# Tile addresses, one load on another queue and two whole iotas in a one-core attention and gated-feed-forward kernel

## The chip, the cores and the metric

The kernel runs on one core of a Trainium2 chip. The metric is the device time of one execution in microseconds (us). Fifteen executions before the change have a median of 226.3 us and lie between 226.01 and 227.61 us. One execution was also recorded by the hardware profiler, and all the lines shown below come from that one.

A core has five engines that work beside each other: PE (TensorE, matrix products; its weight loads are listed as PEld), DVE (VectorE), ACT (ScalarE), POOL (GpSimd) and SP (SyncE, which only issues transfers here). Data moves between the memory of the chip (DRAM) and the on-chip memory (SBUF, 128 partitions) by DMA. A transfer is issued from the instruction stream of SP, ACT or POOL, and then runs on the core's 16 DMA engines. In this kernel every transfer that changes fp32 to bf16 on its way is issued by POOL.

## The reference

Inputs are q, k, v of shape (4 batches, 8 heads, 768 positions, 64), one decay `lam` per head, and three weight matrices. The first half is causal linear attention with decay, in blocks of positions:

```python
intra = einsum('bhic,bhjc->bhij', qb, kb) * Dmask      # lam ** (i - j) where i >= j, else 0
intra = einsum('bhij,bhjd->bhid', intra, vb)
inter = einsum('bhid,bhde->bhie', qb * lam_pow, kv_state)
out[:, :, sl] = intra + inter
kv_state = lam_block * kv_state + einsum('bhsd,bhse->bhde', kb * rev_pow, vb)
```

Its output, as x of shape (3072 tokens, 512), goes through a gated feed-forward layer:

```python
gate = 1 / (1 + exp(-(x @ w_gate)))     # w_gate: 512 x 1536
val = x @ w_val                         # w_val:  512 x 1536
out = (gate * val) @ w_out              # w_out: 1536 x 512
```

## The kernel before

**The steps.** The 768 positions are worked in six steps n = 0 to 5 of 128 positions for all four batches, which makes 512 tokens a step. Attention of a step (`piece_s`, `piece_m`, `piece_a`, and from step 2 the `chunk_` functions) leaves x transposed in the tile `XT`. The feed-forward part (`piece_gv`) then takes twelve slices of 128 columns: for each slice ft four matmuls with `WG` into the gate, four with `WV` into the value (both L484), a sigmoid on ACT and a product on DVE. `piece_po` multiplies the twelve results with `WO` (L519) and stores. From the second half of step 0's feed-forward on, the attention of the next step is put between the matmuls of the present one, so that PE has work while ACT and DVE prepare operands.

**The order.** The scheduling is manual: each engine runs its instructions in the order in which the kernel's lines emit them, and waits only on semaphores for data. So the order of POOL's list is the order of the lines, transfers included.

**The start.** Only step 0 has nothing to overlap with. Its loads are issued in this order:

- SP: batches 0 and 1 of k, as fp32 into the two `h32` tiles (`load_hw`, L150, called on L154 and L155), which DVE then casts to bf16 (`cast_hw`, L289).
- ACT: the decays, `lam_bc`; after that the table for exp and log (L157).
- POOL: q of batches 0 and 1 (L94), the identity and three tables (iotas and selects, up to L170), k of batches 2 and 3, four small iotas into `jn` (L174), a select (L176), q of batch 2, q of batch 3, v of batches 0 and 1, of 2, of 3, and then the weight slices `WG` (L105) and `WV` (L108), alternating; later `WO` (L115) and the loads of steps 1 and 2.

`jn` holds two exponents for each partition, one column for a decay that counts down from the start of a half of 64 rows and one for a decay that counts to its end. It is read only in `tables_late` on ACT (L218, L219).

PE waits in `zeros` (L533, matmuls on zeros) and then takes each batch in turn: `t_` transposes q and k (L263), `e_q` and `e_k` copy the result to SBUF (DVE L271 for q of batch 0, ACT L271 and L284 for the others), `piece_s` makes scores (L306), `piece_m` masks them on DVE (L314), `piece_a` multiplies with v (L337; batch 3 in two parts, L580), and `piece_x` and the lines after it copy to `XT` (ACT L350 and L583, DVE L350 and L584). The first gate product of step 0 is done in two halves, batches 0 and 1 first.

**Later loads.** From step 2 on, q and k are loaded to tiles and then transposed by a transfer from SP (`xbar`, L294). `gate` (L611) puts a one-column copy on POOL that waits for these transposes, and v of the same step is loaded after it.

**Addresses.** Tiles are placed in SBUF by pool, and within a pool in the order in which the code creates them, each rounded up to 32 bytes for a partition. Four constants of 32 bytes each follow the first 16,384 bytes, so that the first tile of the pool `const`, `WG`, starts at byte 16,512, which is 128 past a multiple of 256. `WV`, `WO` and `ident` have sizes that are multiples of 256 and also start 128 past one. The small tiles behind them end with `gates` (4 bytes, rounded to 32) at 64,512, and the pools after `const`, with `kb`, `qb`, `vb`, `h32`, `qt`, `kt`, `XT`, `ob` and all others in them, start at 64,544: every one of these tiles starts 32 past a multiple of 256. A row of 64 bf16 elements that a load of q, k or v writes is 128 bytes long.

Of the kernel before, what the change touches and what calls it, by code (L numbers as in the profile page):

```python
# [8 lines left out]
FP32 = mybir.dt.float32  # L9
BF16 = mybir.dt.bfloat16  # L10
# [6 lines left out]
def kernel(  # L17
# [11 lines left out]
    nc = tc.nc  # L29

    B, H, S, D = q.shape
    C = 128
# [9 lines left out]
    const = ctx.enter_context(tc.tile_pool(name="const", bufs=1))  # L42
# [18 lines left out]
    L = C // 2  # L61
    SYNC = mybir.DependencyInfo(mybir.DependencyClass.Sync, mybir.DependencyReason.DATA)

    WG = const.tile([128, NMT, DFF], BF16, tag="WG")
    WV = const.tile([128, NMT, DFF], BF16, tag="WV")
    WO = const.tile([128, NFT, DM], BF16, tag="WO")
# [15 lines left out]
    def rows_of(u):  # L82
        return slice(u * 64, (u + 1) * 64)

    def load(n, what, b0=0, b1=B):
        sl = slice(n * C, (n + 1) * C)
        for c in what:
            if (c, n) not in T_:
                T_[c, n] = qkv.tile([128, B, H, D], BF16, tag=c + "b", name=c + "b",
                                      bufs=5 if c == "v" else 4)  # L90
            src = {"q": q, "k": k, "v": v}[c]
            nat = b1 if n == 0 or c == "v" else min(b1, NB2)
            if b0 < nat:
                nc.gpsimd.dma_start(  # L94
                    out=T_[c, n][:, b0:nat],
                    in_=src[b0:nat, :, sl, :].rearrange("b h s d -> s (b h) d"))
            if nat < b1:
                m = max(nat, b0)
                for u in range(2):
                    nc.gpsimd.dma_start(  # L100
                        out=T_[c, n][:, m:b1, u::2, :],
                        in_=src[m:b1, 1 - u::2, sl, :].rearrange("b h s d -> s (b h) d"))

    def load_g(f0, f1):
        nc.gpsimd.dma_start(out=WG[:, :, f0 * 128:f1 * 128], in_=wg_r[:, :, f0 * 128:f1 * 128])  # L105

# [25 lines left out]
    jn = const.tile([128, 2], FP32, tag="jn")  # L132
# [14 lines left out]
    def load_hw(c, b, eng):  # L147
        src = {"q": q, "k": k}[c]
        H32[c, b] = hwp.tile([128, H, D], FP32, tag="h32", name="h32")
        eng.dma_start(out=H32[c, b], in_=src[b, :, 0:C, :].rearrange("h s d -> s h d"))  # L150

    T_["k", 0] = qkv.tile([128, B, H, D], BF16, tag="kb", name="kb", bufs=4)
    load_hw("k", 0, nc.sync)
    load_hw("k", 1, nc.sync)  # L154
    nc.scalar.dma_start(out=lam_bc, in_=lam.partition_broadcast(128))  # L155
    load(0, "q", 0, 2)
    nc.scalar.preload_act_table_set("natural_log_exp_and_others")  # L157
    nc.vector.memset(ident, 0.0)
# [5 lines left out]
    for u in range(2):  # L164
# [4 lines left out]
                            pattern=[[1, C]], channel_multiplier=-1)  # L169
    nc.gpsimd.iota(ip1, pattern=[[1, C]], base=1, channel_multiplier=0,  # L170
                   allow_small_or_imprecise_dtypes=True)
    load(0, "k", 2, 4)
    for u, i, base in ((0, 0, -1), (1, 0, -1), (0, 1, L - 1), (1, 1, L - 1)):
        nc.gpsimd.iota(jn[rows_of(u), i:i + 1], pattern=[[0, 1]], base=base, channel_multiplier=-1,  # L174
                       allow_small_or_imprecise_dtypes=True)
    nc.gpsimd.affine_select(out=tri, in_=tri, compare_op=ALU.is_gt, fill=1.0, base=0,  # L176
                            pattern=[[-1, C]], channel_multiplier=1)
# [8 lines left out]
    load_v(4, 5)  # L186
    load_v(5, 6)

    lns = const.tile([128, 2 * H], FP32, tag="lns")
    lnl, lnp = lns[:, 0:H], lns[:, H:2 * H].rearrange("p (i h) -> p i h", i=2)  # L190
    nc.scalar.activation(lnl, lam_bc, AF.Ln)
    for i in range(2):
# [3 lines left out]
    lamq, lamqs = lamq2[:, 0], lamq2[:, 1]  # L196
    for hp in range(HP):
        nc.scalar.activation(lamq[:, hp, :], ip1, AF.Exp, scale=lnp[:, 0, hp:hp + 1])
    pk = const.tile([128, 2, H], FP32, tag="pk")
    kds = const.tile([128, 2, H], FP32, tag="kds")  # L200
    pow_l = const.tile([128, 2 * H], FP32, tag="pow_l")
    dec_l = pow_l[:, H:2 * H].rearrange("p (i h) -> p i h", i=2)
# [10 lines left out]

    def powers(u):
        nc.scalar.activation(mask0[:, u], mask0[:, u], AF.Exp)

    def tables_late():
        nc.scalar.activation(pk[:, 1], lnl, AF.Exp, scale=jn[:, 0:1])  # L218
        nc.scalar.activation(kds[:, 1], lnl, AF.Exp, scale=jn[:, 1:2])  # L219
        nc.scalar.activation(pow_l, lns, AF.Exp, scale=float(L))  # L220
# [38 lines left out]
    def t_(c, n, bs, pool=ps_at, tag="ps"):  # L259
        ps = pool.tile([128, len(bs), HP, C], BF16, name="t" + c, tag=tag)  # L260
        for i, b in enumerate(bs):
            for hp in range(HP):
                nc.tensor.transpose(ps[:, i, hp, :], T_[c, n][:, b, 2 * hp:2 * hp + 2, :], ident)  # L263
        (tqs if c == "q" else tks)[n, bs[0]] = ps

    def e_q(n, bs, eng=None):
        w = len(bs)
        src = tqs[n, bs[0]] if n < FIRST_XBAR else QT[n][:, bs[0]:bs[0] + w]
        t = trsb.tile([128, 2, HP, C], BF16, tag="QS", name="QS")
        if n == 0:  # L270
# [205 lines left out]
    def piece_gv(n, ft):  # L476
# [54 lines left out]
    def zeros(m):  # L531
        for _ in range(m):
            nc.tensor.matmul(zps, lhsT=ST[1, 0][:, 0, 0], rhs=ST[1, 0][:, 0], start=True, stop=True)  # L533

    zeros(9)
    exponents(0)
    powers(0)
    cast_hw("k", 0)
    t_("k", 0, [0])
    e_k(0, [0])  # L540
    exponents(1)
    cast_hw("k", 1)
    zeros(3)
    powers(1)
    t_("q", 0, [0])
    e_q(0, [0], nc.vector)
    t_("q", 0, [1])
# [56 lines left out]
    load(1, "v", 2, 4)  # L604
    load(2, "qk")

    gates = const.tile([128, 2], BF16, tag="gates")

    def gate(n):
        for i, t in enumerate((QT[n], KT[n])):  # L610
# [157 lines left out]
```

## Time and profile before

| what | value |
|---|---|
| median of 15 executions | 226.3 us |
| profiled execution, its own time | 226.36 us |
| its span, first to last instruction | 224.6 us |
| PE busy | 215.2 us, 96% |
| ACT, DVE, POOL busy | 106.3, 104.4, 64.9 us |
| DMA transfers issued by POOL | 82,944 packets, 13.90 MB |
| granted TensorE clock | 1.0 throughout |

The span leaves out 1.76 us of the profiled execution's time. In the lists of instructions below, the columns are the start in us, the time from the first start to the last end, the engine, the line, the operation, what it writes and reads, and the shape; `xN` is the number of instructions put together. Brackets at the end give the idle time of the engine just before, and what ended it. An engine that stands with a `q` (SPq, ACTq, POOLq) is the sequencer that issues transfers. A table by window gives, for each stretch of time, the busy time of each engine with the number of its instructions, the granted clock, the DMA share (the mean number of packets in flight on a DMA engine) and the bytes written per time.

### The profile page before, as it was taken

How to read it: one execution, taken by the hardware profiler on the slowest of the kernel's cores; microseconds unless marked ns; L12 is line 12 of the kernel's file. 1: busy time of each engine (PE TensorE's matmuls, PEld its weight loads, DVE VectorE, ACT ScalarE, POOL GpSimd, SP SyncE). 2: the span in 40 equal slices, each digit the busy share in tenths (PEclk: the TensorE clock that was granted, in tenths of full speed). 3: DMA queues.
4: the chain of work that ended last, by engine and by line, in shares of the span. 5: the costliest groups of instructions: out<-in, count | busy, mean ns of one | idle time of the engine just before them, and what ended most of it. 6: DMA issues, size and time to landing. Idle time of an engine off the chain costs nothing.

```text
span 224.6 us, 5200 instructions
## 1 busy us (share of the span) xinstructions
PE 215.2 (96%) x2178; PEld 105.8 (47%) x2187; DVE 104.4 (46%) x194; ACT 106.3 (47%) x232; POOL 64.9 (29%) x85
## 2 busy tenths in 40 slices
PE   6699999999998999999999999999999999999994
PEld 2453444557444544444544444544444544444443
DVE  4686553439776700676700676800676500333300
ACT  5777434495385342366342366342367342333221
POOL 7998964660076001920490022000000000000000
PEclk9999999999999999999999999999999999999999
DMA  7999999999959999999499959112100012100022
GB/s 111 139 161 182 195 201 178 179 154 143 154 64 158 229 133 260 132 155 141 92 127 207 218 110 83 13 50 93 47 3 0 0 50 96 47 0 0 4 93 95
DMA packets 106008, 25.25 MB, mean 112 GB/s; under 512 B 97152, under 2 KB 103552, under 8 KB 105984
## 3 DMA queue, kind: packets, MB, share of 16 engines
q0 software_dynamic: 82944, 13.90, 83.7%
q1 hardware_dynamic: 22752, 10.95, 22.5%
q8 instruction: 17, 0.28, 0.6%
q10 hardware_dynamic: 288, 0.07, 0.1%
q14 instruction: 7, 0.06, 0.1%
HBM read 28.32 MB, written 6.29 MB: 154 GB/s over the span
## 4 chain that ended last, share of the span: by engine, by line
PE 67%; DMA 22%; POOL 7%; issue 2%; ACT 0%; POOLq 0%; SPq 0%
PE po L519 23%; PE gp L484 20%; PE vp L484 20%; DMA WV<-in_moe_w_val_dram 6%; DMA WO<-in_moe_w_out_dram 6%; DMA kb<-in_k_dram 5%; DMA vb<-in_v_dram 3%; DMA kt<-kb 2%; POOL WG L105 1%; POOL vb L94 1%; PE cp L443 1%; PE op L407 1%; PE op L421 1%; PE sp L383 1%; POOL qb L94 1%
## 5 line engine op out<-in xcount | busy, mean ns | idle before, releaser
L484 PE MATMUL vp<-XT,WV 128*128 128x512 bf16 (+1 forms) x292 | 74.1, 376 | 0.4 <-DMA WV<-in_moe_w_val_dram 0.4
L484 PE MATMUL gp<-XT,WG 128*128 128x512 bf16 (+1 forms) x296 | 74.2, 374 | 0.2 <-DMA WG<-in_moe_w_gate_dram 0.2
L496 ACT ACTIVATE sg<-gp 128x512 bf16<-128x512 f32 x72 | 43.0, 597 | 63.9 <-PE gp L484 63.9
L501 DVE TENSOR_TENSOR ht<-sg,vp 128x512 bf16<-128x512 bf16 x48 | 33.0, 687 | 79.9 <-PE vp L484 77.0
L519 PE MATMUL po<-WO,ht 128*128 128x512 bf16 (+2 forms) x292 | 63.3, 370 | 0.5 <-issue 0.2
L484 PEld LDWEIGHTS <-WV 128*128 128x128 bf16 x292 | 28.5, 98 | 34.0 <-DMA WV<-in_moe_w_val_dram 0.9
L519 PEld LDWEIGHTS <-ht 128*128 128x128 bf16 x300 | 28.2, 98 | 31.9
L484 PEld LDWEIGHTS <-WG 128*128 128x128 bf16 x296 | 28.2, 98 | 31.8 <-DMA WG<-in_moe_w_gate_dram 0.3
L523 ACT COPY ob<-po 128x512 f32<-128x512 f32 (+1 forms) x24 | 13.7, 572 | 38.8 <-PE po L519 38.8
L127 ACT ACTIVATE kd<-kb,kds 128x128 bf16<-128x128 bf16 (+1 forms) x88 | 28.8, 400 | 0.0
L499 DVE TENSOR_TENSOR ht<-sg,vp 128x512 bf16<-128x512 bf16 x24 | 16.5, 687 | 13.6 <-PE vp L484 13.6
L611 POOL COPY gates<-qt 128x1 bf16<-128x1 bf16 x4 | 1.2, 302 | 49.9 <-DMA qt<-qb 49.9
L94 POOL DMA_DIRECT2D vb<-in_v_dram x9 | 11.9, 1334 | 2.5 <-issue 1.8
L314 DVE TENSOR_TENSOR MT<-sp,mask 128x512 bf16<-128x512 f32 x16 | 9.9, 684 | 2.7 <-PE sp L306 2.7
L433 ACT CAST XT<-op 128x512 bf16<-128x512 f32 x16 | 8.2, 599 | 5.0 <-PE op L421 5.0
L393 DVE TENSOR_TENSOR MT<-sp,mask 128x512 bf16<-128x512 f32 x16 | 10.3, 682 | 0.0
L100 POOL DMA_DIRECT2D qb<-in_q_dram x10 | 8.8, 891 | 3.3 <-DMA WO<-in_moe_w_out_dram 3.1
L94 POOL DMA_DIRECT2D qb<-in_q_dram x8 | 8.8, 1102 | 2.0 <-DMA WO<-in_moe_w_out_dram 1.0
L100 POOL DMA_DIRECT2D kb<-in_k_dram x10 | 8.9, 909 | 1.0 <-DMA WG<-in_moe_w_gate_dram 0.6
L533 PE MATMUL zps<-st 128*128 128x512 bf16 x17 | 5.8, 472 | 1.6 <-DVE st L159 1.5
L94 POOL DMA_DIRECT2D kb<-in_k_dram x6 | 7.0, 1172 | 0.5 <-DMA WG<-in_moe_w_gate_dram 0.4
L108 POOL DMA_DIRECT2D WV<-in_moe_w_val_dram x9 | 7.2, 811 | 0.0
(79 smaller groups left out, 114.7 us busy)
## 6 DMA issues: line engine op xcount, KB each, us to landing
out_dram<-ob SPq DMA_DIRECT2D x19, 256.0 KB, 2.0
vb<-in_v_dram POOLq DMA_DIRECT2D x4, 512.0 KB, 7.3
qb<-in_q_dram POOLq DMA_DIRECT2D x6, 256.0 KB, 7.5
kb<-in_k_dram POOLq DMA_DIRECT2D x6, 256.0 KB, 10.6
qb<-in_q_dram POOLq DMA_DIRECT2D x12, 128.0 KB, 8.9
WO<-in_moe_w_out_dram POOLq DMA_DIRECT2D x4, 384.0 KB, 12.2
kb<-in_k_dram POOLq DMA_DIRECT2D x10, 128.0 KB, 10.6
WG<-in_moe_w_gate_dram POOLq DMA_DIRECT2D x4, 256.0 KB, 6.8
```

What stands on the lines that cost most here:

```text
L94: nc.gpsimd.dma_start(out=T_[c, n][:, b0:nat], in_=src[b0:nat, :, sl, :].rearrange("b h s d -> s (b h) d"))
L100: nc.gpsimd.dma_start(out=T_[c, n][:, m:b1, u::2, :], in_=src[m:b1, 1 - u::2, sl, :].rearrange("b h s d -> s (b h) d"))
L127: nc.scalar.mul(KD[n][:, at, i, :], T_["k", n][:, at, i, :], kds[:, min(n // FIRST_XBAR, 1), h:h + 1])
L314: nc.vector.tensor_tensor(out=MT[n, b][:, u], in0=SP[n, b][u], in1=mask0[:, 1 - u if swapped(n, b) else u], op=ALU.mult)
L393: nc.vector.tensor_tensor(out=MT[n, bp][:, u], in0=SP[n, bp][u], in1=mask[:, u ^ bp].unsqueeze(1).to_broadcast([128, 2, HP, L]), op=ALU.mult)
L433: nc.scalar.copy(XT[n][:, c, :, bp * C:(bp + 1) * C], OP[n, c, bp].rearrange("p h j i -> p h (j i)"))
L484: nc.tensor.matmul(ps[:, part], lhsT=W[:, mt, fs], rhs=XT[n][:, part, mt], start=(part is not second and mt == 0), stop=(part is not first ...
L496: nc.scalar.activation(sg, gp.rearrange("p a b -> p (a b)"), AF.Sigmoid)
L499: mul = nc.vector.tensor_mul(HT[n, ft], sg, vp.rearrange("p a b -> p (a b)"))
L501: mul = nc.vector.tensor_mul(HT[n, ft].rearrange("p (b c i) -> p c b i", b=B, c=2), sg.rearrange("p (c b i) -> p c b i", c=2, b=B), vp.rea ...
L519: nc.tensor.matmul(po[:, :c1 - c0], lhsT=HT[n, ft][:, tt * 128:(tt + 1) * 128], rhs=WO[:, ft, c0:c1], start=(ft == 0), stop=(ft == NFT - 1))
L523: (eng.copy if eng is nc.scalar else eng.tensor_copy)(o, po[:, :c1 - c0])
```

## The change

Three things are done, in one diff. First, `lns` and `pk`, two tiles of 64 bytes for a partition, are created ahead of `WG`, and `gates` is widened from 2 to 128 columns, of which still only two are written. `WG`, `WV`, `WO` and `ident` move 128 bytes up, to 16,640 and on, and the pools behind `const` move 224 bytes up, to 64,768; both numbers are multiples of 256. Tiles between them move too: `ip1`, `tri`, `dij` and `neg` to 32 past a multiple, `swap` and `lamq2` to 64 past one, while `kds`, `pow_l`, `mask0` and `mask` stay.

Second, batch 1 of k is issued from ACT, behind the load of the decays and ahead of the table load, and no longer from SP behind batch 0.

Third, `jn` is filled by two iotas over all 128 partitions in the place of four over 64. Each is right for one half of the rows; a new function `chunk_rows`, called behind `powers(1)`, adds 64 to the second half of one column and takes 64 from the first half of the other, with two DVE instructions of 64 partitions and one element.

```diff
+    lns = const.tile([128, 2 * H], FP32, tag="lns")
+    pk = const.tile([128, 2, H], FP32, tag="pk")
     WG = const.tile([128, NMT, DFF], BF16, tag="WG")
...
     load_hw("k", 0, nc.sync)
-    load_hw("k", 1, nc.sync)
     nc.scalar.dma_start(out=lam_bc, in_=lam.partition_broadcast(128))
+    load_hw("k", 1, nc.scalar)
     load(0, "q", 0, 2)
...
-    for u, i, base in ((0, 0, -1), (1, 0, -1), (0, 1, L - 1), (1, 1, L - 1)):
-        nc.gpsimd.iota(jn[rows_of(u), i:i + 1], pattern=[[0, 1]], base=base, channel_multiplier=-1,
+    for i, base in enumerate((-1, C - 1)):
+        nc.gpsimd.iota(jn[:, i:i + 1], pattern=[[0, 1]], base=base, channel_multiplier=-1,
                        allow_small_or_imprecise_dtypes=True)
...
+    def chunk_rows():
+        nc.vector.tensor_scalar_add(jn[rows_of(1), 0:1], jn[rows_of(1), 0:1], float(L))
+        nc.vector.tensor_scalar_add(jn[rows_of(0), 1:2], jn[rows_of(0), 1:2], -float(L))
...
     powers(1)
+    chunk_rows()
     t_("q", 0, [0])
...
-    gates = const.tile([128, 2], BF16, tag="gates")
+    gates = const.tile([128, 128], BF16, tag="gates")
```

More of the change, by code (lines that the diff above doesn't have):

```diff
@@ L187 @@
     load_v(5, 6)
-    lns = const.tile([128, 2 * H], FP32, tag="lns")
     lnl, lnp = lns[:, 0:H], lns[:, H:2 * H].rearrange("p (i h) -> p i h", i=2)
@@ L198 @@
         nc.scalar.activation(lamq[:, hp, :], ip1, AF.Exp, scale=lnp[:, 0, hp:hp + 1])
-    pk = const.tile([128, 2, H], FP32, tag="pk")
     kds = const.tile([128, 2, H], FP32, tag="kds")
```

## The prediction

> **What bounds the kernel now.** I read the chain of waits first, then PE's list of instructions, since PE is busy 96% of the span. PE's list around its last idle moments:
>
> ```profile
> 14.83 0.39 PE L239 MATMUL lqs<-lamq,swap 128*128 128x512 bf16 x1
> 15.27 0.41 PE L580 MATMUL op<-MT,vb 128*64 128x128 bf16 x8
> 15.85 1.05 PE L484 MATMUL gp<-XT,WG 128*128 128x256 bf16 x8 [0.16 <-DMA WG<-in_moe_w_gate_dram]
> ...
> 19.00 1.04 PE L484 MATMUL vp<-XT,WV 128*128 128x512 bf16 x4 [0.38 <-DMA WV<-in_moe_w_val_dram]
> ...
> 70.86 0.73 PE cp L443 x60
> ```
>
> The last line is the chain's: there it changes from transfers to PE, and from 70.86 us to the end it names PE alone (small pieces of issue aside). Behind 15.85 us PE idles 0.38 us ahead of 19.00, 0.78 us ahead of 70.86 (L443 waits there for `vb`) and 0.16 us ahead of 50.26, the last for no transfer. So time can come from two places: the start, where all 15.85 us pass before the first gate product, and at most 0.38 + 0.78 = 1.16 us behind it, for whatever makes a load faster. Everything else is matmuls at a full clock.
>
> What sets 15.85? POOL's list, and the stretches by window (columns after the engines: clock, DMA share, GB/s):
>
> ```profile
> 4.73 0.98 POOL L174 IOTA jn<- 64x1 f32 x4
> 5.78 0.31 POOL L176 TENSOR_SCALAR_AFFINE_SELECT tri<-tri 128x128 f32<-128x128 f32 x1
> 6.04 1.79 POOL L94 DMA_DIRECT2D qb<-in_q_dram  x2
> 7.82 2.91 POOL L94 DMA_DIRECT2D vb<-in_v_dram  x3
> 10.69 0.80 POOL L105 DMA_DIRECT2D WG<-in_moe_w_gate_dram  x1
> ...
> 3.50:4.25 0.75, 0.75 (x3) 0.30 (x2) 0.05 (x1) 0.37 (x3) 0.75 (x2) 1.00 1.26 284
> 8.50:10.00 1.50, 0.96 (x22) 0.70 (x21) 0.94 (x2) 1.26 (x4) 1.50 (x3) 1.00 2.23 142
> 10.00:11.75 1.75, 1.68 (x25) 1.09 (x22) 1.75 (x4) 1.42 (x6) 1.75 (x3) 1.00 1.85 118
> 15.00:16.75 1.75, 1.54 (x18) 1.06 (x18) 1.66 (x4) 0.51 (x2) 1.75 (x4) 1.00 1.81 178
> 25.00:29.00 4.00, 4.00 (x21) 1.82 (x19) 2.34 (x5) 1.19 (x2) 3.21 (x4) 1.00 1.45 196
> 32.20:34.00 1.80, 1.80 (x10) 0.86 (x9) 0.72 (x2) 0.60 (x1) 0.90 (x2) 1.00 1.23 204
> 44.00:49.00 5.00, 5.00 (x37) 2.76 (x36) 2.36 (x4) 3.83 (x9) 4.38 (x5) 1.00 2.44 156
> 58.00:59.00 1.00, 1.00 (x6) 0.41 (x5) 0.02 (x1) 0.60 (x1) 0.00 (x0) 1.00 1.28 290
> ```
>
> The reader is to see that POOL issues the loads of step 0 without a pause from 6.04 us on, one 128 KB (written) batch in 0.9 us, and that just before it spends 0.98 us on the four iotas. The landings follow at a fixed distance: the first `WG` slice is issued at 10.69 and lands 5.1 us later (its tile's answer), at 15.80, and PE starts on it at 15.85. And the DMA engines are not full all the time: a long run of the same 128-byte rows goes at 156 GB/s (44 to 49 us), but 8.5 to 10 us at 142 and 10 to 11.75 us at 118. The holes come to 1.5 x (1 - 142/156) = 0.13 us and 1.75 x (1 - 118/156) = 0.43 us, together 0.56 us.
>
> **Part 1, the addresses.** No instruction is added or taken away; the price is in packets. Is a row that straddles a 256-byte line dearer? Rates give the time of one packet on one of 16 engines, 16 x size / rate. 128-byte rows, every second one across a line (they start at 32 past): 16 x 128 / 156 = 13.1 ns. 256-byte rows of `WG` and `WV`, all across (128 past): 16 x 256 / 178 = 23.0. 512 bytes: 16 x 512 / 196 = 41.8. 1024 bytes of `WO`: 16 x 1024 / 204 = 80.3. From 128 to 1024 bytes this is nearly one straight line, 3.6 ns + 0.075 ns a byte, and on it the half-straddling rows stand no lower than the all-straddling ones. So I cost POOL's loads at zero change. Its ends: a gain up to the 1.16 us that loads still cost PE; a loss of zero, because operands that start at one and the same distance from a line, as all will, meet in L306 already (`KS` and `QS`, both 32 past) and run there at PE's pace, eight in 0.40 us.
>
> Transfers issued by SP move 256-byte pieces: 284 GB/s for `h32` (3.5 to 4.25 us) and 290 for the transposes (58 to 59 us), so 16 x 256 / 284 = 14.4 and 14.1 ns, where POOL's packets, which also read 256 bytes of fp32, take 13.1. If the difference is the straddling, they go up to 16 x 256 / 13.1 = 312 GB/s: 512 KB of `h32` gain 512 KB x (1/284 - 1/312) = 0.17 us, and each transpose of 512 KB about 0.13 us; if not, zero. I take 0.1 us in the sum: half of it for the start, which `h32` opens, or a part of the 0.78 us at 70.86, since the transposes feed `gate` and with it that `vb`.
>
> The Trainium skill, page "DMA: Bandwidth & Descriptors", section "How a descriptor splits into AXI transactions", counts 32-byte beats from the 256-byte line below the start: 5 and 9 beats for our two kinds of 128-byte rows against 8 for the aligned 256-byte fp32 read beside each. By an estimate from that table straddling is hidden behind the read for POOL's loads and shows only where 9 stands against 8, at `h32` and the transposes, which would make the total about 0.1 to 0.2 us; the rates above agree with it.
>
> **Part 2, batch 1 of k from ACT.** SP loses one issue (0.56 us) behind which nothing waits: its next work is the transpose at 54.73. The load moves behind `lam_bc` (ACT's sequencer 0.74 to 1.17 us) and is issued at about 1.2 us, where SP did it at 1.27. On ACT the table load queued behind it slips from 1.21 to about 1.7 and ends at 3.0; the first use of the table waits for `lam_bc` to land and runs at 3.87, so 0.87 us of cover is left of 1.38. If `lam_bc` landed later by x, the logs, the exponents on DVE (4.20) and the mask powers on ACT would slip by x, against 1.1 us of idle ACT ahead of 8.74. POOL's and SP's other transfers pass nothing. Landings: before, batch 0 lands 4.3 us after 0.75 and batch 1 5.1 us after 1.27, at 6.3. Side by side on the same engines both can at worst end with the later of the two. Then the cast of batch 0 (5.26, on DVE ahead of the second set of exponents, 1.16 us) starts at 6.4, and cast, exponents, second cast and the two small additions (0.42 + 1.16 + 0.50 + 0.3) end at 8.8 instead of 7.2, where the copy of q's transposes runs at 8.52 now: +0.3 us on the attention chain. At best batch 1 lands 0.1 us sooner, which nothing waits for, as DVE takes it at 6.68. I take zero at the end.
>
> The same page, section "Issuing engines are not separate DMA queues", says that issuing from several engines saves only sequencer time; by it this edit is worth nothing here, which is what the rows give.
>
> **Part 3, the iotas.** Four cost 0.98 us on POOL, 125 to 384 ns each (their line's answer), for one element a partition, so I take 128 rows to cost as 64. Two cost between 0.36 and 0.6 us: I take 0.5, so everything POOL issues from 6.04 on comes 0.48 us sooner (0.4 to 0.6). Two additions on DVE are new, 64 partitions by one element; the nearest rows are L223 and L226, 64x8, 0.15 and 0.16 us, and L225 with 0.58. Taken as 0.3 us together (1.2 at worst). DVE is idle from 7.18 to 8.52 there (1.34 us, wait for PE's transposes), and they wait for nothing, the iotas being done by 5.3. Behind them on DVE stands the q copy at 8.52; without the cover the 0.3 us would go straight to the scores. ACT's two readers of `jn` run at 9.70.
>
> How much of 0.48 us arrives? The packets of k ahead (issued at 3.54) don't move. If the holes of 0.56 us are POOL issuing too late, packets follow POOL by up to 0.48; if the engines were slow for another reason, only the 0.13 us before 10 us closes. I take 0.4 for `WG`'s landing, 15.80 to 15.40. What is late next: DVE's last mask product for batch 3 ends at 12.31 + 2.49 = 14.80 and its start goes back to q of batches 0 and 1, which is issued at 1.26 and doesn't move; so L580 can come forward from 15.27 to 14.83, 0.44 us and no more. The DVE copies behind it (0.69 for batch 2, 0.42 for L584) then end about 16.0, in time for the second half of the first product. The weights behind keep their order and spacing, so the wait at 19.00 moves with them, and the one at 70.86 too: from 20 to 58 us the engines are full, and earlier by what they began earlier.
>
> **Sum.** Start: -0.4 us. Aligned SP and ACT transfers: -0.1. The rest: 0. That is 226.36 - 0.5 = 225.86 for the profiled execution, which lies 0.06 above the median: 225.8.
>
> **The rivals.** *POOL's issue is not the limit.* The DMA engines set 8.5 to 11.75 us; for it speaks that packets flow without a stop from 4.4 us on, against it the 156 GB/s that the same rows reach later. Then 0.13 us at most arrives, 226.2.
>
> *Alignment counts after all*, in the landing of a transfer and not in its rate. For it: the 118 and 142 GB/s have no shown cause; against it the straight line. Then most of the 1.16 us goes too: 226.3 - 0.4 - 0.8 = 225.1.
>
> *Slower: batch 0 of k becomes the bound.* Two streams share the engines and `lam_bc` is in front of one; `h32` of batch 0, landed at 5.0 now, comes late and pushes the first transposes, ACT's copies and all masks. The chain has 0.44 us of slack at L580 after part 3's gain, and DVE's own 1.3 us ahead of 8.52; working back as in part 2, a landing at 6.3 costs 0.3 us, which that slack swallows, and each us beyond goes through. With the gain of part 3 lost, the kernel is slower by 0.2% only if batch 0 lands after about 7.0 us; at 7.3 the time is about 227.0. Against it: SP's issue of it doesn't move.
>
> **How the numbers follow.** 0.2% (0.45 us) is about what a measurement tells. Forecast case 0.52, between 225.2 and 226.1; issue not the limit 0.20; alignment counts 0.12; slower 0.16. Faster by over 0.45 us, below 225.85: about six tenths of the forecast case, 0.32, and all of the third, so 0.44. Slower 0.15 of the fourth case's 0.16, the rest 0.41. The range takes the third case's 225.1 and goes up to 226.7, short of the fourth.
>
> **What would show it.** POOL's `qb` pair at about 5.55, `WG`'s first slice issued at 10.2 and landed near 15.4, the first gate product at 15.45, and 10 to 11.75 us above 118 GB/s if the holes were POOL's. POOL's packet rates unchanged at 156, 178 and 196 GB/s; `h32` and transposes above 284 and 290 if straddling cost there. I'm wrong if the first gate product stays at 15.8, if PE finds a new wait for weights between 16 and 24 us (they land 0.2 to 0.5 us ahead of use), or if 70.86 moves by more than the start.

## The result, and the profile after

The changed kernel's median is 224.9 us (224.56 to 225.2, 9 runs), beside 226.49 us (45 runs) of the kernel before in the same comparison. The ratio is 0.9927, with a 95% interval of 0.9915 to 0.9939: 0.73% or 1.6 us faster. Forecast were 225.8 us in a range of 225.1 to 226.7, so the time lies below the range. The profiled execution took 224.77 us with a span of 223.0 (before: 226.36 and 224.6).

PE's list of the changed kernel, around the places that the prediction named (lines moved by 4 or 5, L484 is now L488, L580 is L585, L443 is L447):

```profile
7.40 0.62 PE L267 MATMUL tq<-ident,qb 128*128 128x128 bf16 x8 [0.36 <-DMA qb<-in_q_dram]
...
14.74 0.41 PE L585 MATMUL op<-MT,vb 128*64 128x128 bf16 x8 [0.16 <-DMA vb<-in_v_dram]
15.44 1.05 PE L488 MATMUL gp<-XT,WG 128*128 128x256 bf16 x8 [0.29 <-DMA WG<-in_moe_w_gate_dram]
17.19 1.03 PE L488 MATMUL gp<-XT,WG 128*128 128x512 bf16 x4
18.05 1.03 PE L488 MATMUL vp<-XT,WV 128*128 128x512 bf16 x4
...
69.33 0.73 PE L447 MATMUL cp<-vb,kd 64*64 64x64 bf16 x64 [0.21 <-DMA vb<-in_v_dram]
```

The last of these products in the kernel before:

```profile
70.86 0.73 PE L443 MATMUL cp<-vb,kd 64*64 64x64 bf16 x64 [0.78 <-DMA vb<-in_v_dram]
```

Compare starts, not idle times. The first gate product starts at 15.44 instead of 15.85: 0.41 us. The product that stood at 19.00 behind a wait of 0.38 now runs at 18.05 without one: 0.95 us in all, so 0.54 more than the start alone. The multiplication with `vb` starts at 69.33 instead of 70.86: 1.53 us in all, another 0.58, and its idle time went from 0.78 to 0.21. The remaining 0.07 of the 1.6 is spread over the rest. So in this pair of executions the gain has three portions of about half a microsecond, one at the start and two at waits for loads.

POOL's list of the changed kernel:

```profile
4.73 0.23 POOL L176 IOTA jn<- 128x1 f32 x2
5.21 1.89 POOL L96 DMA_DIRECT2D qb<-in_q_dram  x2
7.08 2.91 POOL L96 DMA_DIRECT2D vb<-in_v_dram  x3
9.94 0.80 POOL L107 DMA_DIRECT2D WG<-in_moe_w_gate_dram  x1
```

The two whole iotas take 0.23 us where the four took 0.98, and the loads that POOL issues behind them come 0.74 to 0.83 us sooner (`qb` 6.04 to 5.21, `vb` 7.82 to 7.08, `WG` 10.69 to 9.94). The table by window (columns as above: engines, clock, DMA share, GB/s) of the changed kernel:

```profile
3.50:4.25 0.75, 0.75 (x3) 0.30 (x2) 0.02 (x1) 0.34 (x3) 0.75 (x2) 1.00 1.18 267
8.50:10.00 1.50, 0.98 (x23) 0.64 (x18) 1.20 (x2) 1.12 (x5) 1.50 (x3) 1.00 2.43 155
10.00:11.75 1.75, 1.44 (x18) 0.72 (x18) 1.28 (x3) 1.39 (x3) 1.75 (x3) 1.00 2.44 156
15.00:16.75 1.75, 1.46 (x16) 1.00 (x11) 1.69 (x6) 0.60 (x2) 1.75 (x4) 1.00 1.83 186
25.00:29.00 4.00, 4.00 (x20) 1.82 (x19) 2.18 (x5) 1.58 (x3) 3.06 (x3) 1.00 1.45 196
44.00:49.00 5.00, 5.00 (x50) 2.80 (x47) 1.44 (x4) 4.64 (x13) 3.77 (x4) 1.00 2.45 156
49.00:56.00 7.00, 6.84 (x131) 4.87 (x127) 6.49 (x16) 4.09 (x10) 0.00 (x0) 1.00 2.31 153
```

The two holes that the prediction marked are filled: 142 and 118 GB/s became 155 and 156. The rates of the full stretches did not move: 156 at 44 to 49 us, 196 for the weights at 25 to 29 us (178 and 186 at 15 to 16.75 us). What did move is the last row. The same stretch of the kernel before:

```profile
49.00:56.00 7.00, 6.84 (x140) 4.91 (x140) 5.58 (x14) 4.49 (x12) 0.00 (x0) 1.00 3.24 145
```

There 3.24 packets were in flight on an engine at 145 GB/s, here 2.31 at 153: each packet took longer, for no more bytes. By 16 x share x size / rate, with 128 bytes, an estimate from these rows is 46 ns a packet before and 31 ns after. This row of the kernel before was in my table when I predicted, and I did not use it. The chain of waits shows what came of it. Of the changed kernel, and then of the one before (start, duration, what):

```profile
47.02 9.35 DMA kb<-in_k_dram
56.42 4.94 DMA kt<-kb
61.85 7.43 DMA vb<-in_v_dram
```

```profile
47.84 10.21 DMA kb<-in_k_dram
58.10 4.93 DMA kt<-kb
63.52 7.30 DMA vb<-in_v_dram
```

The last load of k in step 2 starts 0.82 us sooner, about as much as POOL won at `qb` (0.83), and is 0.86 us shorter. Its transposes take the same time as before (4.94 and 4.93) and `vb` 0.13 more, and hand nearly the whole sum on.

### The profile page after: what moved, and what is told of

Its sections match the earlier page's. It is cut to its first block, busy times and chain, and to the rows that moved or that the text cites. A ratio compares the mean times of both kernels' runs of the same rounds, so it can differ in the third digit from the quotient of the medians.

```text
span 223.0 us, 5199 instructions
## 1 busy us (share of the span) xinstructions
PE 215.9 (97%) x2178; PEld 106.0 (48%) x2187; DVE 104.4 (47%) x196; ACT 106.4 (48%) x232; POOL 64.0 (29%) x83
## 3 DMA queue, kind: packets, MB, share of 16 engines
q1 hardware_dynamic: 21712, 10.69, 20.5%
## 4 chain that ended last, share of the span: by engine, by line
PE 67%; DMA 20%; POOL 10%; issue 2%; ACT 0%; POOLq 0%; SPq 0%
PE po L523 23%; PE gp L488 20%; PE vp L488 20%; DMA WO<-in_moe_w_out_dram 6%; DMA kb<-in_k_dram 4%; DMA WV<-in_moe_w_val_dram 4%; DMA vb<-in_v_dram 3%; POOL WG L107 2%; POOL WV L110 2%; DMA kt<-kb 2%; POOL vb L96 1%; PE cp L447 1%; PE op L411 1%; PE op L425 1%; POOL kb L96 1%
## 5 line engine op out<-in xcount | busy, mean ns | idle before, releaser
L488 PE MATMUL gp<-XT,WG 128*128 128x512 bf16 (+1 forms) x296 | 74.2, 374 | 0.3 <-DMA WG<-in_moe_w_gate_dram 0.3
L488 PE MATMUL vp<-XT,WV 128*128 128x512 bf16 (+1 forms) x292 | 74.1, 376 | 0.0
L488 PEld LDWEIGHTS <-WV 128*128 128x128 bf16 x292 | 28.6, 98 | 33.4
L488 PEld LDWEIGHTS <-WG 128*128 128x128 bf16 x296 | 28.1, 98 | 31.9 <-DMA WG<-in_moe_w_gate_dram 1.0
L537 PE MATMUL zps<-st 128*128 128x512 bf16 x17 | 6.5, 516 | 1.6 <-DVE st L161 1.5
```

The source lines that it names most:

```text
L488: nc.tensor.matmul(ps[:, part], lhsT=W[:, mt, fs], rhs=XT[n][:, part, mt], start=(part is not second and mt == 0), stop=(part is not first ...
```

## The experiments

The theory after the result: rows of q, k and v that straddle a 256-byte line cost time in the landing of their loads, and the iotas give POOL 0.8 us; both are needed for the whole gain. Rivals: the iotas alone (the landings only follow POOL), the weights' addresses, the other queue for k, or the addresses of the remaining tiles (`h32`, transposes). Every ratio is against the kernel before on the same chip; none of these kernels leaves out or changes a part of the computation. A profile shows one execution, and single executions of one kernel differ by some tenths of a microsecond, so the medians decide what a part is worth.

### Each part alone

**iota_only**: of the change, the two iotas and the additions behind them.

```diff
-    for u, i, base in ((0, 0, -1), (1, 0, -1), (0, 1, L - 1), (1, 1, L - 1)):
-        nc.gpsimd.iota(jn[rows_of(u), i:i + 1], pattern=[[0, 1]], base=base, channel_multiplier=-1,
+    for i, base in enumerate((-1, C - 1)):
+        nc.gpsimd.iota(jn[:, i:i + 1], pattern=[[0, 1]], base=base, channel_multiplier=-1,
...
     powers(1)
+    chunk_rows()
```

> Only the two whole iotas and the two additions on DVE; all addresses and queues as before. Theory 'landings': the iotas give POOL 0.83 us (qb pair at 5.21 instead of 6.04 us), but the rows of q, k and v still start 32 past a line, so the first q still lands near 8.0 us and the wait ahead of 70.86 us stays: first gate product 0.3 to 0.45 us sooner, the wait at 19 us may go (0.55 us from start to start), total -0.3 to -0.95 us, and the last us of k's landings at 36 to 58 us stay as far behind their packets as before. Rival 'POOL alone': the whole gain of 1.6 us is POOL's earlier issue; total -1.4 us or more.

Measured: 226.80 us, ratio 1.0019 (1.0003 to 1.0034). The iotas alone bring nothing, rather a loss; neither expected gain came, not the theory's 0.3 to 0.95 us either. POOL did issue sooner: its `qb` pair stands at 5.17 instead of 6.04. From PE's list and the table by window of this kernel:

```profile
8.10 0.96 PE L267 MATMUL tq<-ident,qb 128*128 128x128 bf16 x8 [1.31 <-DMA qb<-in_q_dram]
```

```profile
8.50:10.00 1.50, 1.50 (x18) 1.07 (x15) 0.42 (x1) 0.90 (x2) 1.50 (x3) 0.50 3.13 147
10.00:11.75 1.75, 1.55 (x21) 1.32 (x20) 1.61 (x3) 1.00 (x5) 1.75 (x3) 0.53 3.71 148
```

The holes are filled here too (147 and 148 GB/s), but with 3.1 to 3.7 packets in flight instead of 2.4: what POOL issues sooner only queues. The first load of q still lands at 8.06, and the clock column shows half speed in this execution, to which I come back.

**act_only**: of the change, batch 1 of k from ACT's queue.

```diff
-    load_hw("k", 1, nc.sync)
     nc.scalar.dma_start(out=lam_bc, in_=lam.partition_broadcast(128))
+    load_hw("k", 1, nc.scalar)
```

> Only the move of k's batch 1 to ACT's queue. Theory 'landings': nothing, within 0.2 us of before, first q landed at 8.0 us. Rival 'the queue': the first q's landing at 7.36 instead of 8.04 us in the full change comes from here; then the first transposes of q run 0.6 us sooner, yet the loads behind are set by POOL, so at most -0.3 us.

Measured: 226.30 us, ratio 1.0004 (0.999 to 1.0019). Worth nothing, as costed, and as the Trainium skill, page "DMA: Bandwidth & Descriptors", section "Issuing engines are not separate DMA queues", would have it. In its profiled execution the value product of slice 1 stands at 18.46 us without a wait, 0.54 sooner than before, though every address is as before: the portion at 19.00 can come and go without a change of address.

**weights_only**: of the change, `lns` and `pk` made ahead of `WG`, which puts the weights on a line.

```diff
+    lns = const.tile([128, 2 * H], FP32, tag="lns")
+    pk = const.tile([128, 2, H], FP32, tag="pk")
     WG = const.tile([128, NMT, DFF], BF16, tag="WG")
...
-    lns = const.tile([128, 2 * H], FP32, tag="lns")
...
-    pk = const.tile([128, 2, H], FP32, tag="pk")
```

> Only lns and pk ahead of the weights: WG, WV and WO start on a 256-byte line, all later pools stay 32 past one. Theory 'landings': the weight rows are 256 bytes and longer and their landings trailed their packets by 0.3 to 0.5 us already where nothing else disturbs, so no gain, within 0.2 us of before. Rival 'weights': the wait of 0.55 us at 19 us goes with it, -0.5 us.

Measured: 226.49 us, ratio 1.0012 (0.9996 to 1.0029). The weights' addresses bring nothing. PE's list of this kernel has a wait of another size and place:

```profile
15.57 1.05 PE L484 MATMUL gp<-XT,WG 128*128 128x256 bf16 x8 [0.28 <-DMA WG<-in_moe_w_gate_dram]
18.88 1.04 PE L484 MATMUL gp<-XT,WG 128*128 128x512 bf16 x4 [1.39 <-DMA WG<-in_moe_w_gate_dram]
```

Slice 1 of `WG` is waited for here, with 1.39 us of idle time, where before it was slice 1 of `WV`. The start is 0.28 us sooner than before, the value product of slice 1 (19.75, before 19.00) 0.75 later, and the product with `vb` 0.31 later (71.17, after 0.36 us of idle time instead of 0.78). So the time of this one kernel mixes the addresses with a wait that has moved; the last section looks at it, and no_weights below is the cleaner comparison.

**pools_only**: of the change, `gates` widened to 128 columns, which puts every tile of the pools behind it on a line; the weights stay 128 past one.

```diff
-    gates = const.tile([128, 2], BF16, tag="gates")
+    gates = const.tile([128, 128], BF16, tag="gates")
```

> Only the widened gates tile: q, k, v, h32, qt, kt and all tiles of later pools start on a 256-byte line, the weights stay 128 past one. Theory 'landings': the landings in the long run of 128-byte rows trail their last packet by 0.3 to 0.75 us instead of 0.9 to 2.1, the last k of step 2 lands about 1 us sooner, the wait of the v products near 70 us shrinks by 0.5 us or more, the first q lands at 7.4 us; first gate product as before; total -0.5 to -0.9 us. Rival 'straight line' (the prediction): 0 to -0.2 us.

Measured: 225.17 us, ratio 0.9954 (0.9938 to 0.9971), 1.0 us faster, a little more than expected. Table by window and PE's list of this kernel:

```profile
49.00:56.00 7.00, 7.00 (x141) 5.08 (x141) 6.04 (x15) 4.09 (x12) 0.00 (x0) 1.00 2.43 158
```

```profile
7.29 0.62 PE L263 MATMUL tq<-ident,qb 128*128 128x128 bf16 x8 [0.57 <-DMA qb<-in_q_dram]
15.75 1.05 PE L484 MATMUL gp<-XT,WG 128*128 128x256 bf16 x8 [0.28 <-DMA WG<-in_moe_w_gate_dram]
69.55 0.74 PE L443 MATMUL cp<-vb,kd 64*64 64x64 bf16 x64
```

The queueing is gone (2.43 packets in flight at 158 GB/s), q lands 0.8 us sooner although POOL issues as before, and the wait for `vb` near 70 us is gone. The start has won only 0.10 us: the iotas' portion is missing.

### Which addresses

A head's row of q, k or v is 128 bytes, as the tile holds it. Before, the rows start 32 past a 256-byte line, so every second row lies across one. The next kernels move the pools by other amounts.

**pools_64**: all later pools 64 bytes past a line; every second row still lies across one.

```diff
-    gates = const.tile([128, 2], BF16, tag="gates")
+    gates = const.tile([128, 32], BF16, tag="gates")
```

> gates 32 columns wide: every tile of the later pools starts 64 past a 256-byte line, so every second 128-byte row of q, k and v still straddles a line, but all rows start and end on a multiple of 64. Theory 'straddling' (a row over a 256-byte line is written dearer): as before, 0 to -0.2 us, landings trail their packets by 0.8 to 2.1 us. Rival 'small unit' (what costs is a row that starts off a multiple of 64 bytes): as pools_only, -1.0 us, with trails of 0.3 to 0.8 us.

Measured: 226.46 us, ratio 1.0002 (0.9985 to 1.002). Nothing.

**pools_128**: all later pools 128 bytes past a line; no tile on a line, but no 128-byte row across one.

```diff
-    gates = const.tile([128, 2], BF16, tag="gates")
+    gates = const.tile([128, 64], BF16, tag="gates")
```

> gates 64 columns wide: the later pools start 128 past a line, no 128-byte row straddles one, but the 256-byte rows of h32 and every longer row do. Theory 'straddling': as pools_only, -0.8 to -1.1 us, since the rows of q, k and v are the ones that matter; h32 and the transposes alone would be left, at most 0.2 us. Rival 'the whole tile must start on a line': as before.

Measured: 225.20 us, ratio 0.9945 (0.9929 to 0.9962). The whole gain of pools_only, so a tile need not start on a 256-byte line. That it is lines of 256 bytes that the rows must not cross is not shown by this: at 32 and 64 past a line every 128-byte row also lies across a multiple of 128 bytes, at 0 and 128 none does, so lines of 128 bytes would give the same four results. Two other rows bear on it and disagree. The 256-byte rows of `h32`, which lie across a 256-byte line in pools_128 but start at a multiple of 128, land 0.66 and 0.70 us behind their closing packets (explained below) in pools_128, 0.66 and 0.84 in the kernel before, and 0.34 and 0.31 in pools_only, which speaks for 256. The weights' rows, also 128 past a line, cost nothing in time (weights_only and no_weights), which does not. No run separates the two sizes for the rows of q, k and v; "across a line" below means across a 256-byte line, as the edits were planned.

**qkv_only** and, the same kernel once more, **qkv_again**: only q, k and v on a line, the pools behind them moved off it by a tile that nothing uses.

```diff
+    hwp.tile([128, 16], BF16, tag="pad", name="pad", bufs=1)
...
-    gates = const.tile([128, 2], BF16, tag="gates")
+    gates = const.tile([128, 128], BF16, tag="gates")
```

> gates as wide as in the change, and one unused tile of 32 bytes behind the q, k and v tiles, so that only kb, qb and vb start on a line; h32, qt, kt, ob and all others start 32 past one. Theory 'the rows of q, k and v': -0.8 to -1.1 us as pools_only. Rival 'transposes and stores': h32, transposes or stores carry the gain, so at most half of it is left, -0.5 us or less.

Measured: 225.41 us, ratio 0.9977 (0.9954 to 1.0001): its interval reaches from the theory's gain to none, so the kernel was run again.

> The same kernel as qkv_only: only kb, qb and vb on a line. Theory 'the rows of q, k and v': -0.8 to -1.1 us with an interval clear of 1, first q landed at 7.4 us, trails of 0.3 to 0.8 us. Rival 'transposes, h32 and stores': -0.4 us or less.

Measured: 225.25 us, ratio 0.9957 (0.994 to 0.9974).

**rest_only**: the reverse, q, k and v 32 past a line as before and all the other tiles on one.

```diff
+    hwp.tile([128, 112], BF16, tag="pad", name="pad", bufs=1)
```

> kb, qb and vb stay 32 past a 256-byte line, all tiles of the pools behind them (h32, qt, kt, XT, ob and so on) start on one; queue and iotas as before. Theory 'the rows of q, k and v': 0 to -0.2 us, the first q lands near 8.0 us and the landings from 44 to 57 us trail their last packet by 1 to 2 us. Rival 'transposes, h32 and stores': -0.5 us or more.

Measured: 226.25 us, ratio 1.0009 (0.9992 to 1.0025). Nothing. So the rows of q, k and v carry the gain, and the other tiles behind them don't. The same stretch of the table by window in the four kernels, pools_64, pools_128, qkv_again and rest_only in this order:

```profile
49.00:56.00 7.00, 6.84 (x139) 4.93 (x139) 5.76 (x15) 4.30 (x12) 0.00 (x0) 1.00 3.28 143
```

```profile
49.00:56.00 7.00, 6.84 (x139) 5.02 (x139) 6.15 (x15) 4.09 (x11) 0.00 (x0) 1.00 2.47 158
```

```profile
49.00:56.00 7.00, 7.00 (x141) 4.92 (x139) 5.56 (x13) 4.79 (x13) 0.00 (x0) 1.00 2.44 157
```

```profile
49.00:56.00 7.00, 7.00 (x140) 5.03 (x140) 5.93 (x15) 4.13 (x11) 0.00 (x0) 1.00 3.13 148
```

The DMA share sorts them, and all the kernels here, as the times do: 2.3 to 2.5 where no row of q, k or v lies across a line, 3.1 to 3.3 where every second one does. The records of single packets say where the time goes. A load ends with one 4-byte packet on each engine, its closing packet. The table has the time from the start of the last closing packet to the load's landing, in us, for the first load of q and, as a median, for the loads of steps 1 and 2 that are issued from 38 to 49 us; then the time at which the last k of step 2 has landed, and PE's idle time ahead of the product with `vb` near 70 us:

```
                  first q   38 to 49 us   last k landed   idle ahead of vb   rows across a line
before              0.89        1.45          58.04             0.78               yes
iota_only           0.91        1.73          57.80             1.36               yes
act_only            0.83        1.27          57.54             0.59               yes
pools_64            0.91        1.22          57.44             0.47               yes
rest_only           0.33        1.19          57.35             0.48               yes
pools_only          0.30        0.77          56.74             none               no
pools_128           0.30        0.74          56.92             none               no
qkv_again           0.29        0.86          57.24             none               no
no_iota             0.29        0.89          57.13             none               no
changed kernel      0.29        0.71          56.37             0.21               no
```

The last closing packet had started, and the load still was not there for a median of up to 1.7 us. From 44 to 49 us the rate is 155 or 156 GB/s in every kernel, whatever its rows; from 49 to 56 us it is 137 to 148 GB/s with rows across a line and 151 to 158 without. It is not one slow engine: of the sixteen completions that make up a landing, in the loads issued from 38 to 45 us the middle ones already come 0.9 to 1.1 us behind the closing packets in the kernel before and some 0.3 us behind in the changed one. The records point at the writing side. That writes queue is what fits; it is inferred, as I read no record of the writes themselves.

Two rows need a word. The first q of rest_only lands early (7.28 us) with its rows across the line, and nothing is won by it. There `h32` is on a line, and its two loads land at 4.69 and 5.58 us instead of 5.03 and 6.32; that the first q gains by this fits, but no run tried it. And in the profiled executions of qkv_again and no_iota, with no row across a line, the loads from the first v on (issued at 7.82 and 7.86 us) land about 1.4 us behind their closing packets, so that the first gate product starts at 16.77 and 16.65, later than before. In qkv_again fourteen of the sixteen completions of that v are there by 12.79 us, and the last two come at 13.83 and 14.32. So something else can hold up single engines by as much, and what it is stays open. In both kernels the wait for `vb` is gone even so, and both medians are 0.9 to 1.0 us below the kernel before.

### The change without one of its parts

**no_weights**: the changed kernel with `lns` and `pk` back in their places.

```diff
-    lns = const.tile([128, 2 * H], FP32, tag="lns")
-    pk = const.tile([128, 2, H], FP32, tag="pk")
     WG = const.tile([128, NMT, DFF], BF16, tag="WG")
```

> The whole change without lns and pk ahead of WG: weights stay 128 past a line, everything else as in the change. Theory: the weights are worth nothing of their own, so this ends within 0.2 us of the change, 1.5 us under before. Rival 'weights': with the rest out of the way their landings count at the start, where the first products wait for WG: 0.3 to 0.6 us slower than the change.

Measured: 224.75 us, ratio 0.9926 (0.9911 to 0.9941), as the whole change.

**no_act**: the changed kernel with batch 1 of k on SP's queue.

```diff
+    load_hw("k", 1, nc.sync)
     nc.scalar.dma_start(out=lam_bc, in_=lam.partition_broadcast(128))
-    load_hw("k", 1, nc.scalar)
```

> The change with k's batch 1 back on SP (addresses and iotas as in the change). Theory 'addresses and iotas': the queue is worth nothing, 1.4 to 1.7 us under before. Rival 'the queue helps beside the others' (the gain left over between the aligned pools alone, 1.05, and the whole change, 1.6): 1.0 us under before.

Measured: 224.58 us, ratio 0.9922 (0.9896 to 0.9948), as the whole change.

**no_iota**: the changed kernel with the four small iotas.

```diff
-    for i, base in enumerate((-1, C - 1)):
-        nc.gpsimd.iota(jn[:, i:i + 1], pattern=[[0, 1]], base=base, channel_multiplier=-1,
+    for u, i, base in ((0, 0, -1), (1, 0, -1), (0, 1, L - 1), (1, 1, L - 1)):
+        nc.gpsimd.iota(jn[rows_of(u), i:i + 1], pattern=[[0, 1]], base=base, channel_multiplier=-1,
```

> The change with the four small iotas back on POOL (addresses and the queue as in the change). Theory 'addresses and iotas': POOL's 0.8 us can only arrive where rows don't straddle, so without it 1.0 to 1.1 us under before, first q batches issued at 6.0, first gate product near 15.7. Rival 'the queue': 1.5 us under before.

Measured: 225.20 us, ratio 0.9959 (0.9936 to 0.9981). The first gate product, expected near 15.7 us, starts at 16.65 in the profile, for the late v described above. Three kernels with aligned rows and whole iotas (the change, no_weights, no_act) stand at 0.9922 to 0.9927, four with aligned rows and no whole iotas (this one, pools_only, pools_128, qkv_again) at 0.9945 to 0.9959: with aligned rows the iotas are worth some 0.3%, 0.4 to 0.8 us. Alone they were worth nothing. The intervals of single pairs touch, the two groups do not mix.

### The clock after an idle stretch

In iota_only PE idles 1.31 us ahead of 8.10 and then runs at 0.50 to 0.53 until 11.5 us. The kernel before idles as long and keeps its clock. Is this what makes iota_only slow? The single executions speak against it: of the twelve of iota_only five show a mean clock of 0.992, as the profiled one does, with a median of 226.87 us, and the seven at 1.00 have 226.73, still above the 226.31 of the kernel before. More small matmuls by `zeros` fill the idle stretch.

**iota_warm**: iota_only, and seven rounds of `zeros` instead of three.

```diff
-    zeros(3)
+    zeros(7)
     powers(1)
+    chunk_rows()
```

> The two whole iotas alone, as in the earlier run of them that came out 0.4 us slower, with four more matmuls on zeros (seven instead of three) ahead of the first q, so that PE idles about 0.4 us there and not 1.3. Theory 'clock': that run was slow because the granted clock fell to about 0.5 from 8 to 11.5 us behind the idle stretch; now the clock stays full, and the time is 226.3 or below, down to 225.9. Rival 'queueing' (earlier issue makes the landings pile up): still 226.7 to 226.9.

Measured: 226.44 us, ratio 1.0006 (0.9991 to 1.0022), between what the two theories expected. The table by window and PE's list of this kernel:

```profile
10.00:11.75 1.75, 1.62 (x22) 0.91 (x18) 1.75 (x4) 1.39 (x5) 1.75 (x3) 1.00 3.78 148
```

```profile
15.83 1.05 PE L488 MATMUL gp<-XT,WG 128*128 128x256 bf16 x8 [0.19 <-DMA WG<-in_moe_w_gate_dram]
```

**before_warm**: the kernel before with the same.

```diff
-    zeros(3)
+    zeros(7)
```

> The kernel before with seven matmuls on zeros instead of three ahead of the first q, nothing else. Theory 'landings': the landings don't move, so within 0.2 us of before, with fewer executions above 226.8. Rival 'clock': the idle stretch costs the kernel before too, and filling it gives 0.3 us or more.

Measured: 225.92 us, ratio 0.9988 (0.9966 to 1.001). The median lies 0.3 us below the kernel before, which the rival had named, but the interval takes in no change at all, so this pair decides nothing.

In iota_warm, with the clock at 1.00, the iotas without aligned rows bring nothing still: the first gate product starts at 15.83 against 15.85, and 3.78 packets are in flight. So the landings hold the gain back, not the clock. Near 70 us the kernels with the iotas alone even lose: PE waits 1.36 us for `vb` in iota_only and 1.17 in iota_warm, where it was 0.78 before. Why is open.

### Can more be won?

**later_c**: no_weights, with `load(0, "k", 2, 4)` ahead of the iota of `ip1`, and the chunk products and updates of step 2 one slice later, so that `vb` near 70 us is waited for no more.

```diff
-                more[8].append(do(chunk_c, nx, bp, cs))
+                more[8 + late].append(do(chunk_c, nx, bp, cs))
...
-                more[8].append(do(update_0, nx, bp))
+                more[8 + late].append(do(update_0, nx, bp))
...
-                    more[9 + bp].append(do(update_1, nx, bp))
+                    more[9 + late + bp].append(do(update_1, nx, bp))
```

> An attempt at a faster version: the change without the move of the weights, in which step 2's state products, which wait for v near 69 us, stand one slice of columns later, and k of batches 2 and 3 is issued ahead of the last table on POOL. Theory: the wait of 0.2 us near 69 us goes and the first landings come 0.1 to 0.2 us sooner, 0.2 to 0.4 us under the change, 224.5. Rival 'nothing left there': PE's own chain and the landing that a 16 KB instruction fetch delays near 17 to 19 us set the rest, within 0.2 us of the change.

Measured: 224.67 us, ratio 0.9922 (0.9895 to 0.995): no better than the change. PE's list of this kernel:

```profile
14.89 1.05 PE L488 MATMUL gp<-XT,WG 128*128 128x256 bf16 x8 [0.29 <-DMA WG<-in_moe_w_gate_dram]
18.20 1.04 PE L488 MATMUL vp<-XT,WV 128*128 128x512 bf16 x4 [0.53 <-DMA WV<-in_moe_w_val_dram]
70.93 0.74 PE L447 MATMUL cp<-vb,kd 64*64 64x64 bf16 x64
```

The start comes 0.55 us sooner than in the changed kernel, and a wait of 0.53 for `WV` at 18.20 takes it back: this product stood at 18.05 there.

## Why the prediction was wrong

**The step that failed is part 1's "So I cost POOL's loads at zero change".** In its place the addresses are worth 1.0 us (pools_only) to 1.2 (pools_128), and those of q, k and v alone 1.0 (qkv_again), while pools_64 and rest_only bring nothing. The zero was reasoned from rates as "the time of one packet". But 16 x size / rate is the distance from packet to packet, 13.1 ns; with 2.44 in flight on an engine a packet took some 32 ns (2.44 x 13.1), and from 49 to 56 us, with 3.24 in flight, some 46. The rates that the prediction used did stay (156 and 196 GB/s), and they don't show this. What PE waits for is the landing, and 128-byte rows across a line hold that back, in the table of closing packets by 0.3 us (0.86 against 1.19) to 1.0 (0.71 against 1.73). The lines to look at were there before: a DMA share of 3.24 at 145 GB/s (49 to 56 us) beside 2.44 at 156 (44 to 49 us).

**Part 3's "The landings follow at a fixed distance" failed with it.** `WG`'s first slice landed 5.1 us behind its issue before (POOL's loads ahead of it had 4.6 to 6.8), 5.5 in the changed kernel (9.94 to 15.40) and 5.9 in iota_warm (9.88 to 15.78): without aligned rows the landing stayed where it was, however early POOL issued.

**The rival "Alignment counts after all", given 0.12, is what happened**, in the landing, as its heading says. Its 225.1 us came near, its reasons less so. It took the loads' portion as 0.8 of the 1.16 us of idle time, where the starts show 0.54 + 0.58 = 1.12. And the 118 and 142 GB/s that spoke for it were not the addresses: pools_only, with aligned rows, has 131 and 123 GB/s in these two stretches, and the iotas filled them.

**That q of batches 0 and 1 "doesn't move" fell.** It is issued at 1.26 us in both kernels and landed at 7.36 instead of 8.04. The cap of 0.44 us at L580, which rested on it, fell too: that product came forward by 0.53 (15.27 to 14.74). The start still won just 0.41, for `WG` was then the last to come.

**That the wait at 19.00 moves with the weights, "and the one at 70.86 too", fell.** Both shrank. The prediction itself named this sign: 70.86 moving by more than the start. It moved by 1.53.

**The wait at 19.00 was mis-sized.** I took its 0.38 us of idle time as all that it costs. Without a wait such products start 0.86 us apart (17.19 to 18.05 in the changed kernel); before, the one at 19.00 started 1.41 us behind the one ahead of it, so the wait cost 0.55:

```profile
17.59 1.03 PE L484 MATMUL gp<-XT,WG 128*128 128x512 bf16 x4
```

The list gives such a product 1.03 us although the next one starts 0.86 us after it, so the idle time that it shows is not all that a wait costs. That this wait has to do with the addresses is not shown: act_only lost it too.

**The iotas' price was mis-sized, and their worth was not their own.** "Two cost between 0.36 and 0.6 us: I take 0.5": they took 0.23, and POOL won 0.83 us at `qb`, not 0.48. The forecast of the start, 15.45 us, was met to 0.01 (15.44), `WG` landing at 15.40 as forecast, and that was luck: the slice was issued at 9.94 instead of 10.2 and then took 5.5 us instead of 5.1. Nor would other executions meet it: no_act, no_weights and later_c, equal in time to the change, start at 15.12, 15.22 and 14.89. And it was met with aligned rows: iota_warm has the iotas without them and starts at 15.83, pools_only and pools_128 have the rows without the iotas and start at 15.75 and 15.55.

**Aligned SP and ACT transfers, 0.1 us: not shown.** rest_only stands at 1.0009. With `h32` on a line and both loads on SP the rate in 3.5 to 4.25 us is 283 (pools_only) and 285 GB/s (rest_only), beside 284 before, where I had looked for more (the 267 of the changed kernel go with ACT's queue: act_only has 260), and the last transposes of step 2 took 4.94 us beside 4.93. The two `h32` loads do land 0.34 and 0.74 us sooner in rest_only, and the time did not follow.

**Part 2 at zero was right**, by act_only (1.0004) and no_act. The table load slipped to 1.68 us as worked out, and nothing waited for it. The slower rival, batch 0 of k becoming late, did not come: it landed at 4.81 us, before at 5.03.

**The additions on DVE** took 0.15 us each at 7.37 and 7.55, inside its idle time, as costed.

The Trainium skill, page "DMA: Bandwidth & Descriptors", section "How a descriptor splits into AXI transactions", gives by its rule 5 and 9 beats for the two kinds of rows. My estimate from it hid them behind the 8 beats of the read. Measured, the rows cost 1.0 to 1.2 us (0.9954, 0.9945, 0.9957), so the measurement decides: the rule is worded for what a transaction reads, and the rows are what these loads write.

Open are four things: whether the line that counts for the rows of q, k and v has 256 or 128 bytes, why the loads fall behind only in some stretches (44 to 49 us looks alike in all kernels), what held up single engines in qkv_again and no_iota, and why the iotas alone lengthen the wait near 70 us.

## What to carry to other kernels

Before a load is called free, read its DMA share beside its rate, and its landing beside its last packet: more packets in flight at the same or a lower rate is a queue, and what waits for the landing pays for it. Lay 128-byte rows so that they start at a multiple of 128 bytes (0 and 128 past a 256-byte line gained here, 32 and 64 did not), and judge an edit that issues loads sooner together with what limits their landing, since either one alone can be worth little or nothing. Price a wait by the distance from start to start, not by the idle time that the list shows, and don't take a wait in one profile for a part of the gain before a second kernel shows it.

## What the runs showed of the hardware

**A load waits for its last DMA engine.** In the kernel before, fifteen of the sixteen completions of slice 1 of `WV` are there by 18.02 us and the last comes at 18.96, 1.41 us behind the closing packets; PE waits for it at 19.00. What fits is one long packet: the trace has 17 packets of 16 KB on the queue listed as "instruction", each of 0.9 to 1.5 us, and one of them starts at 16.89 us and takes 0.96. In weights_only one starts at 16.78, and slice 1 of `WG` lands at 18.83, which PE waits for; in later_c slice 1 of `WV` lands at 18.15, with a wait of 0.53. In the changed kernel it starts at 16.57, and slice 2 of `WG` lands at 18.80 and is wanted at 18.92: no wait. So a part of the portion at 19.00 is a matter of how the start falls. This was read from the times of the packets and not tried by an edit of its own, and qkv_again has late engines from 13 us on, ahead of any such packet.

**The clock halved after little idle time.** In iota_only's profiled execution it was 0.50 from 8.21 to 11.63 us, after 1.31 us without a matmul, while the kernel before, with the same idle time, kept 1.00. The Trainium skill, page "TensorE: Matmul & The Clock Gate", section "What's actually happening", speaks of free-running windows of about 3.4 us, one idle for the clock to halve and one busy for it to return; the 3.4 us at half speed agree with it, the 1.31 us of idle time are less than such a window.

**Two iotas over 128 partitions took 0.23 us, four over 64 took 0.98.** One took 0.13 to 0.38 us over 64 partitions and 0.15 or 0.16 over 128, so the width did not show in the price of one.
